# Two layers of cached attention and MLP on one core: most of V's weighting moved from TensorE to VectorE and ScalarE in the first layer

## The chip, the cores and the metric

One core of one Trainium2 chip. The metric is the device time of one execution in microseconds (us). The kernel before takes 677.72 us, the median of three runs (677.35 to 677.88).

## What is computed

One token of width 512 goes through attention, an MLP, the same attention and the same MLP. All weights and caches are float32, and both layers use the same ones.

```
q = (layernorm(x) @ wq) in 32 heads of 128
p = softmax(q . k_cache / sqrt(128)) over 4096 cached positions
o = p . v_cache
x = x + o @ wo
h = gelu(layernorm(x) @ w1 + b1)         # 512 -> 1376
x = x + h @ w2 + b2                      # 1376 -> 512
```

k_cache and v_cache hold 32 heads x 4096 x 128 values, 67 MB each; they don't fit on the core, so each layer reads most of them from HBM.

## The kernel before, in words

**Groups.** The 32 heads go in 8 groups of 4. A group's K and its V are 8.4 MB each (128 partitions x 16,384 values, `BLOCK`), cut into 8 chunks of 2,048 columns (`NC`). Layer 0 takes the groups 0 to 7, layer 1 the groups 7 to 0, so that what lies in SBUF at the end of layer 0 can be used again.

**A group in layer 0** (the loop at L399):
- K is loaded as one transfer, and `scores` (L215) multiplies it with the queries z on TensorE (PE), 8 chunks x 4 heads, all into one PSUM bank, pS.
- `softmax` (L219 to L235) takes maxima and exponentials on VectorE (DVE) and ScalarE (ACT), turns the weights on PE and copies them to `pt` (L229).
- V is loaded as one transfer, and `values` (L243) multiplies it with pt on PE: for each chunk and head the four 128-column blocks of pt against 512 columns of V. Only the diagonal blocks of what comes out in pO are wanted.
- `scaled_out` (L247 to L252) turns pO on DVE, adds up the diagonal blocks and scales.
- `head_out` (L271) multiplies with the group's rows of wo on PE and adds up all groups in one PSUM row, pB.
- `queries` (L205 to L210) makes z of the next group: DVE multiplies the four parts of wq with x and adds them, in place; eight small matmuls sum over the partitions, and a copy puts the result into z.

**Buffers and queues.** All transfers go through SyncE's queue (SP) in program order (`load`, L87); a transfer is issued when its buffer is free, and those behind it wait with it. K and V rotate through three blocks of SBUF: V of a group goes where this group's predecessor had its K, and K of the next group but one goes where this group had its V. wo of a group and wq of the next come as one pair of 2.1 MB into a single place (`PAIR`), behind V; the next pair waits until `queries` and `head_out` have read the old one. Otherwise the framework orders each engine's work by its own estimate of what is ready, except for instructions that `pin` keeps in program order.

**The end of layer 0.** In group 7 V comes in pieces (4, 2, 1 chunks and the last). wo, w1 in two parts and w2 in four follow. `scaled_out_last` treats the last chunk alone. Then comes `mlp`: mean and variance (`mean_of`, `rstd_of`, four small matmuls each), the hidden layer in three thirds (L297; places in PSUM `pH`), a transpose (L309), GELU, and 11 chunks of w2 (L349). The last part of w2 and pieces of layer 1's K and wq are issued behind the chunks of w2 whose places they take (`follow`). `idle` (L374) issues matmuls whose result nobody reads; they keep PE busy where it would wait. `WARM` = 4 of them stand ahead of the hidden layer, and `FILL` = 3 behind the chunks 4 to 7.

Of the kernel before, what the change touches and what calls it, by code (L numbers as in the profile page):

```python
# [17 lines left out]
P = 128  # L18
# [3 lines left out]
G = 8  # L22
# [33 lines left out]
VAR_AT = 1  # L56
WARM = 4


@with_exitstack  # L60
def decode_layers(ctx: ExitStack, tc: tile.TileContext, k, v, w, w1, w2, out):
# [85 lines left out]
    pW = pS[:, 3 * P :], pB[:, :P]  # L147
    pH = (pS, pS[:, P:], pS[:, 2 * P :]), (pS, pB[:, P:], pS[:, P:])
    pM, pN = pO[:, 2 * P : 3 * P], pO[:, 3 * P :]
# [18 lines left out]

    def minus_mean(s, at):
        for j in range(J):  # L170
            nc.tensor.matmul(at[32 * j : 32 * j + 32], negmean.to_broadcast([P, 32]), s, start=True, stop=True)  # L171
        return at

    def mean_of(xs, s, at):
        nm = minus_mean(s, at)
# [5 lines left out]
    def rstd_of(ss, at):  # L181
        nv = minus_mean(ss, at)
# [19 lines left out]

    def queries(n, xc, wt, at, t=None):
        t = wt[:, 0, :] if t is None else t
        pin(nc.vector.tensor_scalar(t, wt[:, 0, :], xc[:, 0:1], None, op0=ALU.mult))  # L205
        for c in range(1, 4):
            nc.vector.scalar_tensor_tensor(t, wt[:, c, :], xc[:, c : c + 1], t, op0=ALU.mult, op1=ALU.add)  # L207
        for j in range(J):
            nc.tensor.matmul(at[:, j : j + 1], t[:, P * j : P * (j + 1)], one, start=True, stop=True)  # L209
        nc.vector.tensor_copy(zq[:, :, C - 1], at[:, :J])  # L210
        return zq
# [29 lines left out]
    def values(i, pt, vt, c, of=C):  # L241
        for j in range(J):
            nc.tensor.matmul(pO[32 * j : 32 * j + 4, :], pt[:, j, c, :], by_head(vt)[:, j],  # L243
                             start=(i == 0), stop=(i == of - 1))

    def scaled_out(rl, ot):
        nc.vector.transpose(ot[:, :512], pO)  # L247
# [3 lines left out]
        nc.vector.tensor_reduce(o, diag, axis=AX.X, op=ALU.add)  # L251
        nc.vector.tensor_scalar(on, o, rl, None, op0=ALU.mult)  # L252
        return on
# [13 lines left out]

    def head_out(on, wt, n):
        for d in range(4):
            if n < G - 1:  # L270
# [12 lines left out]
    def mlp(xs, s, w1_t, w2_t, xb, rows, fill, follow):  # L283
# [7 lines left out]
        def hidden(i):  # L291
            at, first = hs[i], W1_AT[i]
            n = min(32 * HIDDEN[i][1], FJ) - 32 * HIDDEN[i][0]
            for c in range(4):
                for j in range(J):
                    f = first + n * (J * c + j)
                    pin(nc.tensor.matmul(at[32 * j : 32 * j + 2, :n], xs[:, c, :], w1_t[:, f : f + n],  # L297
                                         start=(c == 0), stop=(c == 3)))
                if i == 0 and c == VAR_AT:
                    rstd.append(rstd_of(ss, pN[:, 1:2]))  # L300
                    if fill is None:
                        nc.gpsimd.tensor_tensor(nmr, nm_s, rstd[0], op=ALU.mult)
                        nc.gpsimd.tensor_scalar(cb[:, late:], colsum[:, late:], nmr, None, op0=ALU.mult)
                        nc.gpsimd.tensor_tensor(cb[:, late:], cb[:, late:], b1c[:, late:], op=ALU.add)

# [22 lines left out]
        rstd = []  # L328
        if fill is not None:
            for _ in range(WARM):  # L330
                idle(fill, pO, 2 * P)
# [44 lines left out]
    for layer in range(2):  # L376
        order = list(range(G)) if layer == 0 else list(range(G))[::-1]
        if layer == 0:
            nm, ss, xc = mean_of(xs, s, pN[:, 0:1])
            z = queries(0, xc, wq_first, pO)  # L380
# [12 lines left out]
        xc_l = small("xc_l", 4)  # L393
        r = rstd_of(ss, pN[:, 1:2])
        nc.vector.tensor_copy(xc_l, xc)
# [3 lines left out]
        for n, g in enumerate(order):  # L399
            first, final = n == 0, n == G - 1  # L400

            k_home, v_home = ((2 * n + i) % 3 * BLOCK for i in (1, 2))
# [17 lines left out]
            else:  # L420
                tiles = stream("k", g, HALVES if layer == 1 and final else WHOLE, k_home)
            for c, t in tiles:
# [37 lines left out]
            else:  # L460
                for c, t in stream("v", g, WHOLE, v_home):
                    for i in range(KEPT - 1):
                        if layer == 0 and n == G - 2 and c == (STAY + U * i) // NC:
                            nc.scalar.copy(pK[i], t[:, STAY // U % J + i - J * (c - STAY // NC), :])
                    values(c, pt, t, c)

# [114 lines left out]
```

## Time and profile before

| | us |
|---|---|
| median of three runs | 677.72 |
| the profiled execution | 677.01 |
| its span, first to last instruction | 675.2 |
| busy in it: PE / DVE / ACT | 398.3 / 115.0 / 27.4 |

In the profile PE's weight loads stand apart from its matmuls (PEld), and an f32 matmul shows as two instructions. L215 is line 215 of the kernel. A line of a group tells the engine, what is written and read, the shapes, the count, the busy time, the mean time of one in ns, and the idle time ahead of them with what ended it. The chain of waits follows the work that ended last back to its start. SPq is SyncE's queue: its rows tell when a transfer was issued. The busy time of an engine counts only where others wait for it.

### The profile page before, as it was taken

To read this page: it belongs to the slowest core of one execution; us is meant where nothing else is said; L and a number is where in the kernel's file an instruction comes from. 1 tells how busy PE (TensorE), PEld (TensorE's weight loads), DVE (VectorE), ACT (ScalarE), POOL (GpSimd) and SP (SyncE) were. 2 spreads that over 40 slices of the span, in tenths; PEclk is the share of its full clock that TensorE was granted. 3 is DMA by queue.
4 is the path that set the end of the run, shared out by engine and by line. 5 is a ranking of instruction groups with operands and counts; after the bars stand their busy time and mean duration, and the time that the engine had idled before them with its cause. 6 is when DMAs were issued, how large, how long until landed. Compare 5 with 4: busy or idle time off the path is not lost.

```text
span 675.2 us, 6725 instructions
## 1 busy us (share of the span) xinstructions
PE 398.3 (59%) x3004; PEld 108.3 (16%) x3004; DVE 115.0 (17%) x369; ACT 27.4 (4%) x57; POOL 5.0 (1%) x24
## 2 busy tenths in 40 slices
PE   1544564475545745456498987574355544755697
PEld 1101111111111111111125321111011111111123
DVE  3012110120021201212013322120121011201212
ACT  0010000000000000001011200000000000000010
POOL 1000000000000000000000000000000000000000
PEclk9968876797587856887699998886797678865989
DMA  9999999999999999999999999999999999999996
GB/s 375 435 436 435 436 435 435 413 453 432 427 432 419 447 435 436 431 435 432 417 413 366 393 430 433 432 435 436 431 432 435 433 435 404 451 432 421 432 410 254
DMA packets 10836, 285.34 MB, mean 423 GB/s; under 512 B 1204, under 2 KB 1208, under 8 KB 3384
## 3 DMA queue, kind: packets, MB, share of 16 engines
q1 hardware_dynamic: 10808, 284.92, 98.7%
q8 instruction: 23, 0.38, 0.2%
q14 instruction: 5, 0.04, 0.0%
HBM read 284.92 MB, written 0.00 MB: 422 GB/s over the span
## 4 chain that ended last, share of the span: by engine, by line
PE 41%; DMA 37%; another core or an unknown queue 15%; DVE 4%; ACT 1%; issue 1%; ACTq 0%; SPq 0%; DVEq 0%
DMA arena<-in_v 34%; PE pO L243 19%; PE pS L215 12%; PE pB L271 4%; DMA arena<-in_w 2%; PE pO L209 1%; PE pO L227 1%; PE pS L374 1%; ACT arena L225 1%; DVE smalls L219 1%; DVE arena L247 1%; PE pO L374 1%; PE pO L349 1%; PE pS L297 0%
## 5 line engine op out<-in xcount | busy, mean ns | idle before, releaser
L215 PE MATMUL pS<-arena,smalls 128*8 128x512 f32 x1024 | 141.7, 705 | 121.8 <-DMA arena<-in_k 121.2
L243 PE MATMUL pO<-arena,pt 128*4 128x512 f32 x1008 | 143.3, 710 | 80.7 <-DMA arena<-in_v 80.3
L215 PEld LDWEIGHTS pS<-arena,smalls 128*8 128x8 f32 x1024 | 29.5, 100 | 218.5 <-issue 197.8
L271 PE MATMUL pB<-arena,smalls 128*1 128x512 f32 x112 | 52.0, 608 | 20.1 <-DVE smalls L252 15.9
L243 PEld LDWEIGHTS pO<-arena,pt 128*4 128x4 f32 x1008 | 28.2, 96 | 182.3 <-issue 181.2
L219 DVE TENSOR_REDUCE smalls<-pS 128x1 f32<-128x512 f32 x16 | 11.1, 692 | 255.8 <-PE pS L215 255.8
L247 DVE STREAM_TRANSPOSE arena<-pO 128x512 f32<-128x512 f32 x16 | 11.5, 717 | 220.8 <-PE pO L243 220.8
L227 PE MATMUL pO<-ident,arena 128*128 128x128 f32 x64 | 12.7, 331 | 37.9 <-ACT arena L225 37.6
L225 ACT ACTIVATE arena<-pS,smalls 128x512 f32<-128x512 f32 x16 | 12.4, 778 | 534.8 <-DVE smalls L224 534.8
L207 DVE SCALAR_TENSOR_TENSOR arena<-arena,smalls 128x512 f32<-128x512 f32 x45 | 33.8, 752 | 1.6
L271 PEld LDWEIGHTS pB<-arena,smalls 128*1 128x1 f32 x112 | 8.5, 85 | 63.3 <-issue 35.6
L209 PE MATMUL pO<-smalls,arena 128*128 128x1 f32 x120 | 16.6, 259 | 3.3 <-DVE arena L207 3.3
L209 PEld LDWEIGHTS pO<-smalls,arena 128*128 128x128 f32 x120 | 15.3, 200 | 15.5 <-DVE arena L207 13.8
L227 PEld LDWEIGHTS pO<-ident,arena 128*128 128x128 f32 x64 | 8.2, 163 | 51.8 <-ACT arena L225 46.4
L374 PE MATMUL pS<-arena,ident 128*8 128x512 f32 (+1 forms) x34 | 14.2, 517 | 0.5 <-DVE pt L309 0.5
L374 PE MATMUL pO<-arena,ident 128*8 128x512 f32 (+1 forms) x34 | 12.5, 492 | 0.4 <-DVE smalls L289 0.4
L205 DVE TENSOR_SCALAR arena<-arena,smalls 128x512 f32<-128x512 f32 x15 | 7.2, 480 | 2.8 <-DMA arena<-in_w 2.8
L349 PE MATMUL pO<-arena,smalls 128*1 128x128 f32 x176 | 6.8, 272 | 0.6 <-ACT smalls L323 0.4
L210 DVE COPY smalls<-pO 128x4 f32<-128x4 f32 x15 | 2.5, 165 | 25.7 <-PE pO L209 25.7
L231 DVE STREAM_TRANSPOSE smalls<-smalls 128x32 f32<-128x32 f32 x16 | 3.4, 212 | 17.5 <-ACT arena L225 17.5
L171 PE MATMUL pO<-smalls 128*32 128x1 f32 x64 | 2.2, 184 | 7.0 <-DVE smalls L165 6.5
L297 PE MATMUL pS<-arena,smalls 128*2 128x128 f32 (+1 forms) x160 | 5.2, 259 | 0.5 <-DVE pt L309 0.5
(92 smaller groups left out, 100.9 us busy)
## 6 DMA issues: line engine op xcount, KB each, us to landing
arena<-in_w SPq DMA_DIRECT2D x14, 2048.0 KB, 33.3
arena<-in_k SPq DMA_DIRECT2D x4, 4096.0 KB, 27.8
arena<-in_v SPq DMA_DIRECT2D x2, 4096.0 KB, 38.8
arena<-in_k SPq DMA_DIRECT2D x3, 2048.0 KB, 14.0
arena<-in_v SPq DMA_DIRECT2D x2, 2048.0 KB, 42.0
arena<-in_w SPq DMA_DIRECT2D x4, 1024.0 KB, 15.3
arena<-in_v SPq DMA_DIRECT2D x3, 1024.0 KB, 54.0
arena<-in_w SPq DMA_DIRECT2D x6, 512.0 KB, 10.2
```

The costliest lines, as they stand in the source:

```text
L205: pin(nc.vector.tensor_scalar(t, wt[:, 0, :], xc[:, 0:1], None, op0=ALU.mult))
L207: nc.vector.scalar_tensor_tensor(t, wt[:, c, :], xc[:, c : c + 1], t, op0=ALU.mult, op1=ALU.add)
L209: nc.tensor.matmul(at[:, j : j + 1], t[:, P * j : P * (j + 1)], one, start=True, stop=True)
L215: nc.tensor.matmul(pS[32 * j : 32 * j + C, :], z[:, j, C - 1 - c : 2 * C - 1 - c], kt[:, j, :], start=(c == 0), stop=(c == C - 1))
L219: nc.vector.tensor_reduce(mx[:, 0:1], pS, axis=AX.X, op=ALU.max)
L225: nc.scalar.activation(p, pS, AF.Exp, bias=bias[:, 0:1], scale=sc, accum_out=mx[:, 0:1])
L227: nc.tensor.transpose(pT[:, b].rearrange("p j r -> p (j r)"), p[:, P * b : P * (b + 1)], ident)
L243: nc.tensor.matmul(pO[32 * j : 32 * j + 4, :], pt[:, j, c, :], by_head(vt)[:, j], start=(i == 0), stop=(i == of - 1))
L247: nc.vector.transpose(ot[:, :512], pO)
L271: nc.tensor.matmul(pB[0:1, :], on[:, d : d + 1], wt[:, d, :], start=n == 0 and d == 0, stop=n == G - 2 and d == 3)
L349: pin(nc.tensor.matmul(pM[32 * j : 32 * j + 1, :], g[:, c - b0 : c - b0 + 1], w2_t[c][:, P * j : P * (j + 1)], start=(c == 0), stop=(c == ...
L374: pin(nc.tensor.matmul(at[:C, :n], ident[:, :C], t[:, 0, :n], start=True, stop=True))
```

## The change

- In layer 0, groups 0 to 5, `values` does only the chunks 6 and 7 of V on PE. Chunks 0 to 3 are multiplied by their weights on DVE (one product over 2,048 columns each, in place), chunks 4 and 5 on ACT (32 small products each of 128 columns, 16 a chunk). `add_weighted` sums the six on DVE in one strided reduction, and four matmuls of one row add the result to pO.
- In layer 0, groups 0 to 6, `head_out` sums over wo's four parts on DVE and needs one matmul in place of four.
- In layer 0, from group 0 to 6, `queries` sums over the partitions by one matmul that gives the result on all of them; DVE picks the diagonal by a product with the identity and a reduction. In groups 0 to 5 this comes ahead of the rest of the weighting.
- K of the last group of layer 0 comes in two halves.
- At the start, mean and variance of layer 0 take one matmul each in place of four.
- In the first MLP the variance is computed ahead of the hidden layer, two warming matmuls stand in place of four, and the second third of the hidden layer lies in pO in place of pS.

```
-WARM = 4
+WARM = 2
+VECTOR, SCALAR = 6, 2
...
-    pH = (pS, pS[:, P:], pS[:, 2 * P :]), (pS, pB[:, P:], pS[:, P:])
+    pH = (pS, pO, pS[:, 2 * P :]), (pS, pB[:, P:], pS[:, P:])
...
-    def minus_mean(s, at):
+    def minus_mean(s, at, whole=False):
+        if whole:
+            nc.tensor.matmul(at, negmean.to_broadcast([P, P]), s, start=True, stop=True)
+            return at
...
-    def queries(n, xc, wt, at, t=None):
+    def queries(n, xc, wt, at, t=None, short=False):
...
+        if short:
+            nc.tensor.matmul(at, one.to_broadcast([P, P]), t, start=True, stop=True)
+            own = t.rearrange("p (j d) -> p j d", j=J)
+            nc.vector.tensor_tensor(own, at.rearrange("p (j d) -> p j d", j=J),
+                                    ident[:, None, :].to_broadcast([P, J, P]), op=ALU.mult)
+            nc.vector.tensor_reduce(zq[:, :, C - 1], own, axis=AX.X, op=ALU.add)
+            return zq
...
+    def weighted(pt, at, a, b):
+        own = arena[:, at + NC * a : at + NC * b].rearrange("p (r j d) -> p r j d", j=J, d=DH)
+        for i in range(a, b):
+            t = own[:, 4 * (i - a) : 4 * (i - a + 1)]
+            if i >= vec - SCALAR:
+                for r in range(4):
+                    for j in range(J):
+                        nc.scalar.activation(t[:, r, j], t[:, r, j], AF.Copy, scale=pt[:, j, i, r : r + 1])
+                continue
+            weight = pt[:, :, i, :].rearrange("p j b -> p b j")[:, :, :, None].to_broadcast([P, 4, J, DH])
+            nc.vector.tensor_tensor(t, t, weight, op=ALU.mult)
+
+    def add_weighted(at, n, t):
+        nc.vector.tensor_reduce(t, arena[:, at : at + NC * n].rearrange("p (r m) -> p m r", m=U),
+                                axis=AX.X, op=ALU.add)
+        for j in range(J):
+            nc.tensor.matmul(pO[32 * j : 32 * j + 1, :P], one, t[:, P * j : P * (j + 1)], start=False, stop=True)
...
     def head_out(on, wt, n):
+        if layer == 0 and n < G - 1:
+            t = wt[:, 0, :]
+            nc.vector.tensor_scalar(t, t, on[:, 0:1], None, op0=ALU.mult)
+            for d in range(1, 4):
+                nc.vector.scalar_tensor_tensor(t, wt[:, d, :], on[:, d : d + 1], t, op0=ALU.mult, op1=ALU.add)
+            nc.tensor.matmul(pB[0:1, :], one, t, start=n == 0, stop=n == G - 2)
+            return
...
-                if i == 0 and c == VAR_AT:
+                if i == 0 and c == VAR_AT and fill is None:
                     rstd.append(rstd_of(ss, pN[:, 1:2]))
...
         if fill is not None:
+            rstd.append(rstd_of(ss, pN[:, 1:2]))
             for _ in range(WARM):
                 idle(fill, pO, 2 * P)
...
+            vec = VECTOR if layer == 0 and n < G - 2 else 0
...
-                tiles = stream("k", g, HALVES if layer == 1 and final else WHOLE, k_home)
+                tiles = stream("k", g, HALVES if final else WHOLE, k_home)
...
-                    values(c, pt, t, c)
+                    if c >= vec:
+                        values(c - vec, pt, t, c, C - vec + (vec > 0))
+            if vec:
+                weighted(pt, v_home, vec - SCALAR, vec)
+                weighted(pt, v_home, 0, 2)
...
+            if vec:
+                z = queries(n + 1, xc_l, wq_next, pS, short=True)
+                weighted(pt, v_home, 2, vec - SCALAR)
+                add_weighted(v_home, vec, wq_next[:, 1, :])
             on = scaled_out_last(rl, pt, last_v, others) if final else scaled_out(rl, ot)
...
-            if not final and not (layer == 1 and n == 0):
-                z = queries(n + 1, xc_l, wq_next, pO, ot[:, :U] if layer == 0 and n == G - 2 else None)
+            if not final and not vec and not (layer == 1 and n == 0):
+                z = queries(n + 1, xc_l, wq_next, pO, ot[:, :U] if layer == 0 and n == G - 2 else None, layer == 0)
```

More of the change, by code (lines that the diff above doesn't have):

```diff
@@ L172, in minus_mean, with mean_of @@
         return at
-    def mean_of(xs, s, at):
-        nm = minus_mean(s, at)
+    def mean_of(xs, s, at, whole=False):
+        nm = minus_mean(s, at, whole)
         xc, sq, ss = small("xc", 4), small("sq", 4), small("ss")
@@ L179, in mean_of, with rstd_of @@
         return nm, ss, xc
-    def rstd_of(ss, at):
-        nv = minus_mean(ss, at)
+    def rstd_of(ss, at, whole=False):
+        nv = minus_mean(ss, at, whole)
         ve, r = small("ve"), small("rstd")
@@ L298, in hidden @@
                                          start=(c == 0), stop=(c == 3)))
-                if i == 0 and c == VAR_AT:
+                if i == 0 and c == VAR_AT and fill is None:
                     rstd.append(rstd_of(ss, pN[:, 1:2]))
[L301 to L304, printed above, removed]
+                    nc.gpsimd.tensor_tensor(nmr, nm_s, rstd[0], op=ALU.mult)
+                    nc.gpsimd.tensor_scalar(cb[:, late:], colsum[:, late:], nmr, None, op0=ALU.mult)
+                    nc.gpsimd.tensor_tensor(cb[:, late:], cb[:, late:], b1c[:, late:], op=ALU.add)
         def turned(i):
@@ L378, in decode_layers @@
         if layer == 0:
-            nm, ss, xc = mean_of(xs, s, pN[:, 0:1])
+            nm, ss, xc = mean_of(xs, s, pN[:, 0:1], True)
             z = queries(0, xc, wq_first, pO)
@@ L393, in decode_layers @@
         xc_l = small("xc_l", 4)
-        r = rstd_of(ss, pN[:, 1:2])
+        r = rstd_of(ss, pN[:, 1:2], layer == 0)
         nc.vector.tensor_copy(xc_l, xc)
```

## The prediction

> **What bounds the kernel now.** I read the page's line of DMA first, then the stages by windows, then one group of layer 0 in order of time, then the hand-over from layer 0 to its MLP. The page and the windows (columns: length, busy time of PE, its weight load, DVE, ACT, POOL, then the granted PE clock, the DMA share and GB/s):
>
> ```profile
> span 675.2 us, 6725 instructions
> PE 398.3 (59%) x3004; PEld 108.3 (16%) x3004; DVE 115.0 (17%) x369; ACT 27.4 (4%) x57; POOL 5.0 (1%) x24
> PEclk9968876797587856887699998886797678865989
> DMA  9999999999999999999999999999999999999996
> GB/s 375 435 436 435 436 435 435 413 453 432 427 432 419 447 435 436 431 435 432 417 413 366 393 430 433 432 435 436 431 432 435 433 435 404 451 432 421 432 410 254
> 4.00:340.00 336.00, 176.63 (x1116) 44.26 (x1120) 50.13 (x148) 10.62 (x21) 0.92 (x4) 0.78 1.00 433
> 356.00:384.00 28.00, 25.30 (x396) 12.41 (x396) 10.66 (x47) 3.56 (x8) 1.79 (x6) 1.00 0.97 371
> 660.00:675.20 15.20, 10.62 (x279) 6.11 (x271) 5.03 (x22) 0.62 (x3) 1.50 (x5) 0.96 0.60 238
> ```
>
> From 4 to 340 us, all of layer 0's attention, the 16 DMA engines are full and move 433 GB/s while PE is busy for 177 of 336 us. Bytes are what this kernel pays for. Past the start it gets less than that rate in two places alone: the tail after 660 us, which is layer 1's and stays as it is, and the first MLP with the start of layer 1, where 28 us at 371 in place of 433 GB/s lose 28 x 62/433 = 4.0 us. So a faster layer 0 attention is worth nothing as such, and the most that the edit of the first MLP can bring is 4.0 us.
>
> One group of layer 0 (timeline; start, length):
>
> ```profile
> 44.65 9.36 PE L243 MATMUL pO<-arena,pt 128*4 128x512 f32 x64 [5.85 <-DMA arena<-in_v]
> 55.34 3.59 PE L271 MATMUL pB<-arena,smalls 128*1 128x512 f32 x8 [1.33 <-DVE smalls L252]
> 59.94 0.33 SPq L87 DMA_DIRECT2D arena<-in_w  x1
> 60.32 0.42 SPq L87 DMA_DIRECT2D arena<-in_k  x1
> 69.98 8.65 PE L215 MATMUL pS<-arena,smalls 128*8 128x512 f32 x64 [10.06 <-DMA arena<-in_k]
> 78.70 0.69 DVE L219 TENSOR_REDUCE smalls<-pS 128x1 f32<-128x512 f32 x1 [18.59 <-PE pS L215]
> 82.16 0.25 DVE L229 COPY pt<-pO 128x128 f32<-128x128 f32 x1
> 89.34 3.60 PE L243 MATMUL pO<-arena,pt 128*4 128x512 f32 x16 [7.30 <-DMA arena<-in_v]
> ```
>
> V of group 0 is there at 44.65, V of group 1 at 89.34: a period of 44.7 us here, about 43.6 in the mean (18.9 MB at 433 GB/s). At 59.94 SP issues the next pair of wo and wq, once the queries have released the old pair; behind it in the same queue stands the next K but one, which overwrites this group's V. Both then wait their turn behind V of group 1, which lands 29 us later. That lead is the cover under which the first half of the change moves.
>
> **The change, part by part.** The prices (columns: busy us, mean ns of one, idle before):
>
> ```profile
> L207 DVE SCALAR_TENSOR_TENSOR arena<-arena,smalls 128x512 f32<-128x512 f32 x45 | 33.8, 752 | 1.6
> L205 DVE TENSOR_SCALAR arena<-arena,smalls 128x512 f32<-128x512 f32 x15 | 7.2, 480 | 2.8 <-DMA arena<-in_w 2.8
> L219 DVE TENSOR_REDUCE smalls<-pS 128x1 f32<-128x512 f32 x16 | 11.1, 692 | 255.8 <-PE pS L215 255.8
> L222 DVE TENSOR_REDUCE smalls<-smalls 128x1 f32<-128x8 f32 x16 | 2.6, 161 | 0.6
> L251 DVE TENSOR_REDUCE smalls<-arena 128x4 f32<-128x16 f32 x16 | 2.9, 179 | 0.5
> L247 DVE STREAM_TRANSPOSE arena<-pO 128x512 f32<-128x512 f32 x16 | 11.5, 717 | 220.8 <-PE pO L243 220.8
> L252 DVE TENSOR_SCALAR smalls<-smalls 128x4 f32<-128x4 f32 x16 | 3.7, 230 | 0.6
> L165 DVE SCALAR_TENSOR_TENSOR smalls<-pt,smalls 128x4 f32<-128x4 f32 x3 | 0.5, 163 | 0.1
> L165 DVE SCALAR_TENSOR_TENSOR smalls<-arena 128x4 f32<-128x4 f32 x1 | 0.2, 164 | 3.1 <-DMA arena<-in_w 3.1
> L464 ACT COPY pK<-arena 128x512 f32<-128x512 f32 x5 | 2.7, 582 | 7.9 <-DMA arena<-in_v 7.9
> L323 ACT ACTIVATE smalls<-smalls 128x4 f32<-128x4 f32 (+1 forms) x6 | 1.2, 207 | 37.6 <-DVE smalls L322 36.6 <-DVE smalls L317 1.0
> ```
>
> *Groups 0 to 5, counted from the landing of V.* L219 against L222: 504 more elements for 531 ns, so 1.05 ns an element over a fixed 0.15 us. No row shows a product of two SBUF tensors of 2,048 elements. By that slope a weighted chunk is 0.15 + 2,048 x 1.05 ns = 2.3 us; the upper bound is four of L207, 3.0 us. I take 2.3, since a slope drops the fixed part that L207 carries each time.
> - Chunks 0 and 1 on DVE: 4.6 us. By then wo and wq have come (2.1 MB, 4.8 us after V); wait 0.3.
> - Queries: 0.48 + 3 x 0.752 = 2.74, as before. The one product over all 512 columns is two of L271's eight instructions, 3.59/4 = 0.9, and takes the place of the eight small ones; then a product with the identity and a reduction over 512 elements, 2 x 0.7 = 1.4, in place of a small copy. z comes 1.2 us later than it could, but K of the next group lands only at +25 (69.98 less 44.65): no cost. Were K early, it would cost those 1.2 us.
> - Chunks 2 and 3: 4.6.
> - Chunks 4 and 5 on ACT beside that: 32 instructions of 128 elements. Between 207 ns (4 elements) and 582 ns (512) that is about 0.30 each, 9.6 us; at 582 each, 18.6. DVE asks for them at +14.6, so nothing, or 4 us at the bound.
> - The sum over six chunks, 12,288 elements whose neighbours lie 2,048 bytes apart. This is the disputed cost, R. At 1.05 ns it is 12.9 us. The nearest strided row is L251, which reads 16 elements 516 bytes apart in 179 ns where eight adjacent ones take 161: if the whole excess over a fixed 153 ns lies in the elements, 1.6 ns each and R = 20; if the eight further ones carry it, 18/8 = 2.25 ns and R = 27.6. Against that, L165 takes 163 ns with a strided first input (x3) and 164 with an adjacent one. And L251 writes four results where L222 writes one, which may be its excess. I take 12.9, by L165.
> - Four small matmuls 0.4, then L247, L251 and L252, 1.1; wo as a chain on DVE 2.74 and one product 0.9, against 3.59 on PE before.
>
> Sum: 4.6 + 0.3 + 2.7 + 0.9 + 1.4 + 4.6 + R + 0.4 + 1.1 + 2.7 + 0.9 = 19.6 + R = 32.5 us. So SP issues the next pair at 44.65 + 32.5 = 77.2 in place of 59.94, with K but one behind it. Who waits? Nobody, while V of group 1 is still coming, until 89.3. The deadline: a piece of w2 below, issued into a nearly empty queue, takes 4.8 us for 0.79 MB, that is 1.8 us of bytes and 3.0 of way. So the pair must be issued by 89.3 - 3.0 = 86.3, which is 41.6 after V: R may be 22.0 us. DVE itself: its part ends at +31.6, the next softmax (78.70 to 82.41, 3.7 us) begins at +34 and ends at +38, the next V comes at +44.7. Both fit, with 9 and 6 us to spare. PE, relieved of 48 of 64 value matmuls, gains nothing, because it waits for DMA on both sides.
>
> [...]
>
> *Group 6* keeps its values on PE. Its wo chain comes ahead of the queries on DVE, so z(7) is ready at about 326 instead of 323; K of group 7, now in two halves, has its first at 332.08 - 9.7 = 322.3.
>
> *The end of layer 0* (chain of waits; then two loads by issue and landing):
>
> ```profile
> 332.08 9.06 PE pS L215 x64
> 341.17 0.70 DVE smalls L219
> 358.01 0.33 DVE pt L504
> 359.24 1.49 PE pO L374 x7
> 361.14 0.99 PE pS L297 x29
> 363.58 0.87 PE pO L349 x32
> 367.87 1.30 PE pS L374 x6
> 369.19 0.84 PE pO L349 x24
> ```
>
> ```profile
> L87 SPq DMA_DIRECT2D arena<-in_w x1: 431/431/431, 322.3 to 322.3; - x1
> DMA to landing us min/median/max: 37.9/37.9/37.9
> L87 SPq DMA_DIRECT2D arena<-in_w x1: 328/328/328, 364.3 to 364.3; - x1
> DMA to landing us min/median/max: 4.8/4.8/4.8
> ```
>
> With the halves, 32 scores are done before K's end and only half remains: 4.5 us of the 9.06 go. But V's pieces and wo come when they come. wo comes 2.1 MB, 4.8 us, ahead of w1's first part, which lands at 322.3 + 37.9 = 360.2; wo is there at 355.4, and 32 small matmuls like those of L297 (0.99) follow, so L504 can't start before about 356.4, against 358.01: 1.6 us gained. The hidden layer's first third needs w1: 360.3 instead of 361.14, 0.8 us. Two warming matmuls fewer and the variance ahead of them cost nothing, since PE waits for w1 there. The second third, now in another PSUM bank, doesn't wait for the transpose; but w2's first megabyte lands 2.4 us behind w1, at 362.6, so L349 starts 0.8 us earlier. Its end releases the last part of w2 (issued 364.3, landed 369.1), also 0.8 earlier. Now the rest of w1 (0.7 MB, at 364.3) and w2's next two pieces (0.5 MB each, to 366.7) are late in its place. These were issued in time before and are bound by bytes; PE used them as they came. So the next chunks end at 367.8, and the six filling matmuls hold PE till 367.8 + 1.3 = 369.1, against 369.19. **0.1 us is left of 0.8.**
>
> *The start* loses six tiny matmuls while K's 8.4 MB are coming: nothing.
>
> Sum against the profiled run, 677.01 us (span 675.2, 1.8 around it): 677.01 - 0.1 = 676.9. The median of the three runs, 677.72, lies 0.7 above the profiled one, so the forecast is **677.6**. Some 0.2%, 1.35 us, is what can be told from no change.
>
> **The rivals.**
> *DVE overruns (slower, 0.20).* If the strided sum takes over 22 us, 1.8 ns an element, the pair of weights is issued into an empty queue, and from then DVE sets the period. For: L251's 2.25. Against: L165's 163. At R = 27.6 the chain is 47.2 us; the first gap is 47.2 - 41.6 = 5.6. Then DVE goes from its end (0.9 us before the issue) through the softmax into the next V: a period of 47.2 - 0.9 + 3.7 = 50.0 against 43.6, five times 6.4. Together 38 us: 715. At R = 24: 2.0 + 5 x 2.8 = 16: 694.
> *The clock drops in the MLP (0.10).* Fewer warming matmuls leave PE nearly idle from 358 to 360. The page's PEclk falls to 5 to 8 in slices where PE waits for DMA. At half clock the matmuls from L297 to L349 (0.99, as much again and 0.87) cost 2.9 us more, less the 0.8 gained: up to +2.1, 678.6 to 679.8. Decides if the clock falls between 357 and 361.
> *The MLP's gain holds (faster, 0.10).* If DMA uses the earlier issues to refill a third to all of the 4.0 us: 676.3 down to 673.7. Against: the chain above, bound by landings and fillers.
>
> **How the numbers follow.** Forecast 0.60, at 677.6 give or take 0.5. Faster by over 0.2%: the third rival, 0.10. Slower: the first, 0.20, and 0.04 of the second above 679.1. Within: 0.60 and 0.06. The range starts at 675.7, half of the 4.0 us won back, and goes to 682.0, over the second rival's end and an overrun of 0.7 us in each of six groups (R = 22.7). Outside stay 0.03 below and 0.17 of the overrun above.
>
> **What would show it.** The strided reduction: 12.9 us for one (about 20 would still pass, 27 not). DVE some 275 us busy in place of 115 (26 us in each of six groups), PE about 340 (398, less 48 x 0.146 = 7.0 in each of six groups and 2.7 in each of seven heads). SP issues of the pair near 77, then every 43.6 us; V of the groups landing as before; 433 GB/s from 4 to 340. Scores of group 7 end near 336; L504 near 356.4; L297 at 360.3; the last L349 still near 369.1. A gap in GB/s inside layer 0 would make me wrong on DVE, an L349 ending before 368.5 on the MLP.

## The result and the profile after

| | before | after |
|---|---|---|
| median | 677.5 (676.94 to 677.88, 6 runs) | 725.65 (724.41 to 728.35, 6 runs) |
| ratio, 95% interval | | 1.0715 [1.0703, 1.0727] |
| profiled execution, its span | 677.01, 675.2 | 728.35, 725.9 |

The change costs 48 us. The forecast was no change, 677.6 us in a range of 675.7 to 682.0; the measured time lies 44 us above that range.

The page of after: its span, busy times, GB/s by slice, the share of each engine in the chain of waits, the two groups that carry the loss, and the products on ACT (line numbers from here on are those of the kernel that the rows belong to; scores are now L226, values on PE L254, softmax starts at L230):

```profile
span 725.9 us, 6315 instructions
PE 353.3 (49%) x2664; PEld 93.2 (13%) x2664; DVE 316.1 (44%) x434; ACT 84.0 (12%) x249; POOL 5.0 (1%) x24
GB/s 406 404 460 408 415 438 451 185 473 408 232 415 448 177 460 408 231 456 354 255 433 409 315 391 430 436 420 444 441 423 441 407 457 420 444 423 423 431 413 235
DVE 35%; DMA 34%; PE 28%; issue 2%; ACT 1%; ACTq 0%; DVEq 0%; SPq 0%
L272 DVE TENSOR_REDUCE arena<-arena 128x512 f32<-128x12288 f32 x6 | 124.1, 20678 | 0.0
L275 PE MATMUL pO<-arena,smalls 128*1 128x128 f32 x48 | 7.1, 395 | 171.8 <-DVE arena L272 171.8
L265 ACT ACTIVATE arena<-arena,pt 128x128 f32<-128x128 f32 x192 | 56.7, 387 | 12.6 <-DMA arena<-in_v 7.0 <-DVE pt L240 5.5
```

The row of GB/s was level in layer 0 and now has five holes, of 177 to 255. One strided sum takes 20.7 us, and over the six groups PE stands 172 us ahead of the four small products of each group that add its result to pO. From here on "the sum" is `add_weighted`'s on DVE, "the sum's products" are these four matmuls, and "the head's product" is the one matmul of `head_out`.

One group of after in order of time, from V of group 0 to V of group 1 (start, length, ..., the idle time ahead):

```profile
44.51 6.70 DVE L268 TENSOR_TENSOR arena<-arena,pt 128x2048 f32<-128x2048 f32 x3 [5.75 <-DMA arena<-in_v]
53.72 1.53 DVE L211 SCALAR_TENSOR_TENSOR arena<-arena,smalls 128x512 f32<-128x512 f32 x2
55.17 20.68 DVE L272 TENSOR_REDUCE arena<-arena 128x512 f32<-128x12288 f32 x1
75.77 0.74 DVE L211 SCALAR_TENSOR_TENSOR arena<-arena,smalls 128x512 f32<-128x512 f32 x1
76.56 2.07 PE L213 MATMUL pS<-arena,smalls 128*128 128x512 f32 x2
79.91 0.65 DVE L217 TENSOR_REDUCE smalls<-arena 128x4 f32<-128x512 f32 x1
83.84 1.01 PE L305 MATMUL pB<-arena,smalls 128*1 128x512 f32 x1 [4.69 <-DVE arena L304]
84.67 9.76 PE L226 MATMUL pS<-arena,smalls 128*8 128x512 f32 x61
85.74 0.33 SPq L88 DMA_DIRECT2D arena<-in_w  x1
94.52 0.69 DVE L230 TENSOR_REDUCE smalls<-pS 128x1 f32<-128x512 f32 x1 [10.73 <-PE pS L226]
98.26 2.29 DVE L268 TENSOR_TENSOR arena<-arena,pt 128x2048 f32<-128x2048 f32 x1
...
139.49 0.33 SPq L88 DMA_DIRECT2D arena<-in_w  x1
351.37 0.33 SPq L88 DMA_DIRECT2D arena<-in_w  x1
```

Two things are not where the prediction had them. The last step of the queries (L211 at 75.77) stands behind the sum, so z is ready at 80.6 (end of L217). And the next group's scores begin at 83.9, with the head's product (L305), although their K, behind the same bytes, had come by 69.98 in before. They end at 94.4, the softmax follows, and the weighting of V, which landed at 89.3, starts at 98.26. Weighting, sum, head, scores and softmax are one row, that is, each waits for the one ahead of it: 53.75 us from 44.51 to 98.26. SP issues the pair at 85.74 and, five groups later, at 351.37: (351.37 - 85.74)/5 = 53.1 us a group in place of 43.6. Five times 9.5 us are 47.5, of a loss of 48.

### The profile page after: what moved, and what is told of

Same layout as the page of the kernel before. It is cut to its first block, busy times and chain, and to the rows that moved or that the text cites. A ratio compares the mean times of both kernels' runs of the same rounds, so it can differ in the third digit from the quotient of the medians.

```text
span 725.9 us, 6315 instructions
## 1 busy us (share of the span) xinstructions
PE 353.3 (49%) x2664; PEld 93.2 (13%) x2664; DVE 316.1 (44%) x434; ACT 84.0 (12%) x249; POOL 5.0 (1%) x24
## 4 chain that ended last, share of the span: by engine, by line
DVE 35%; DMA 34%; PE 28%; issue 2%; ACT 1%; ACTq 0%; DVEq 0%; SPq 0%
DMA arena<-in_v 32%; DVE arena L272 17%; PE pO L254 10%; PE pS L226 10%; DVE arena L268 7%; DMA arena<-in_w 2%; DVE arena L211 2%; DVE arena L304 2%; PE pS L213 2%; PE pB L305 2%; PE pS L412 1%; DVE smalls L230 1%; PE pO L387 1%; DVE arena L215 1%; DVE arena L278 1%
## 5 line engine op out<-in xcount | busy, mean ns | idle before, releaser
L226 PE MATMUL pS<-arena,smalls 128*8 128x512 f32 x1024 | 146.4, 699 | 55.6 <-DMA arena<-in_k 53.5
L254 PE MATMUL pO<-arena,pt 128*4 128x512 f32 x720 | 105.4, 711 | 44.0 <-DMA arena<-in_v 41.1
L272 DVE TENSOR_REDUCE arena<-arena 128x512 f32<-128x12288 f32 x6 | 124.1, 20678 | 0.0
L230 DVE TENSOR_REDUCE smalls<-pS 128x1 f32<-128x512 f32 x16 | 11.1, 692 | 194.9 <-PE pS L226 194.9
L236 ACT ACTIVATE arena<-pS,smalls 128x512 f32<-128x512 f32 x16 | 12.4, 777 | 521.7 <-DVE smalls L235 521.7
L278 DVE STREAM_TRANSPOSE arena<-pO 128x512 f32<-128x512 f32 x16 | 11.4, 713 | 123.2 <-PE pO L254 123.2
L265 ACT ACTIVATE arena<-arena,pt 128x128 f32<-128x128 f32 x192 | 56.7, 387 | 12.6 <-DMA arena<-in_v 7.0
L268 DVE TENSOR_TENSOR arena<-arena,pt 128x2048 f32<-128x2048 f32 x24 | 53.9, 2285 | 5.8 <-DMA arena<-in_v 5.8
L226 PEld LDWEIGHTS pS<-arena,smalls 128*8 128x8 f32 x1024 | 29.7, 97 | 157.7 <-issue 135.5
L211 DVE SCALAR_TENSOR_TENSOR arena<-arena,smalls 128x512 f32<-128x512 f32 x45 | 33.7, 749 | 1.1
L254 PEld LDWEIGHTS pO<-arena,pt 128*4 128x4 f32 x720 | 19.6, 95 | 113.1 <-issue 108.2
L309 PE MATMUL pB<-arena,smalls 128*1 128x512 f32 x56 | 26.9, 625 | 10.8 <-DVE smalls L283 6.6
L305 PE MATMUL pB<-arena,smalls 128*1 128x512 f32 x14 | 12.4, 988 | 32.4 <-DVE arena L304 32.4
L304 DVE SCALAR_TENSOR_TENSOR arena<-arena,smalls 128x512 f32<-128x512 f32 x21 | 15.8, 751 | 0.7
L238 PEld LDWEIGHTS pO<-ident,arena 128*128 128x128 f32 x64 | 7.3, 150 | 51.9 <-ACT arena L236 46.5
L213 PE MATMUL pS<-arena,smalls 128*128 128x512 f32 x12 | 12.5, 1141 | 0.4
```

The costliest lines, as they stand in the source:

```text
L213: nc.tensor.matmul(at, one.to_broadcast([P, P]), t, start=True, stop=True)
L226: nc.tensor.matmul(pS[32 * j : 32 * j + C, :], z[:, j, C - 1 - c : 2 * C - 1 - c], kt[:, j, :], start=(c == 0), stop=(c == C - 1))
L238: nc.tensor.transpose(pT[:, b].rearrange("p j r -> p (j r)"), p[:, P * b : P * (b + 1)], ident)
L265: nc.scalar.activation(t[:, r, j], t[:, r, j], AF.Copy, scale=pt[:, j, i, r : r + 1])
L268: nc.vector.tensor_tensor(t, t, weight, op=ALU.mult)
L272: nc.vector.tensor_reduce(t, arena[:, at : at + NC * n].rearrange("p (r m) -> p m r", m=U), axis=AX.X, op=ALU.add)
```

## The experiments

Three theories stand in the first expectations. The first, the row (A): the next group's scores stand on PE behind the weighted sum and the head, so that the steps of a group can't overlap. The second, the queries (B): only the late z costs. The third, VectorE's work (C): the added work is too much in any order. The deadline in what follows is the prediction's estimate: the pair of the first group has to be issued by 86.3 us, or DMA runs dry; how far ahead of it the pair comes is the lead. Unless something else is said, a kernel computes the whole reference.

**The price of the strided sum.** The kernel before, with one more reduction over the 12,288 values of V in each of the groups 0 to 5; its result is not used.

```
+            if layer == 0 and n < 6:
+                src = arena[:, v_home : v_home + 6 * NC]
+                view = (src.rearrange("p (m r) -> p m r", m=1), src.rearrange("p (r m) -> p m r", m=U),
...
+                pin(nc.vector.tensor_reduce(made, view, axis=AX.X, op=ALU.add))
```

> The kernel before, with one more reduction on DVE in each of the groups 0 to 5, in the time in which DVE is idle behind the queries; it reads 12,288 values of V and its result is not used. Group 0: all adjacent, one result. Group 1: 512 results of 24 adjacent values. Group 2: 512 results of 24 values 2,048 bytes apart, as in the change. Groups 3, 4, 5: 512 results of 24 values 8, 16 and 32 bytes apart. The prediction's price (1.05 ns an element) gives 12.9 us for all six. If distance costs, as the shape of the four diagonal blocks suggested (1.6 ns an element), groups 0 and 1 take 12.9 and group 2 takes 20.7, and the other three tell from which distance on. If the number of results costs, groups 1 to 5 all take about 20.7 and group 0 takes 12.9. The time of the kernel should stay within 1 us of before, since DMA is ahead by 29 us.

In the kernel the groups 1 and 2 are the other way round than the expectation says. By group: all adjacent with one result; 24 values 2,048 bytes apart for each of 512 results; 24 adjacent; 8 bytes apart; 16; 32. The timeline of this kernel, start and length:

```profile
59.05 12.94 DVE L511 TENSOR_REDUCE arena<-arena 128x1 f32<-128x12288 f32 x1
105.45 21.17 DVE L511 TENSOR_REDUCE arena<-arena 128x512 f32<-128x12288 f32 x1
147.76 12.94 DVE L511 TENSOR_REDUCE arena<-arena 128x512 f32<-128x12288 f32 x1
191.78 12.94 DVE L511 TENSOR_REDUCE arena<-arena 128x512 f32<-128x12288 f32 x1
235.78 22.17 DVE L511 TENSOR_REDUCE arena<-arena 128x512 f32<-128x12288 f32 x1
279.78 22.31 DVE L511 TENSOR_REDUCE arena<-arena 128x512 f32<-128x12288 f32 x1
```

Distance is the price: 12.94 us, 1.05 ns an element, at 4 and 8 bytes; 22.17 and 22.31 us, 1.8 ns, at 16 and 32; 21.17 us, 1.7 ns, at 2,048. The number of results cost nothing: 12.94 us for one as for 512. The step lies between 8 and 16 bytes; what makes it, the rows don't show. The time was 677.41 us (one run): 13 to 22 us more of DVE in each group, with nobody waiting, cost nothing. That speaks against the third theory.

**z early.** After, with the query steps, the weighting of the chunks 2 and 3 (`between`), the two last steps of the queries and the strided sum pinned on DVE in this order.

```
-            nc.vector.scalar_tensor_tensor(t, wt[:, c, :], xc[:, c : c + 1], t, op0=ALU.mult, op1=ALU.add)
+            pin(nc.vector.scalar_tensor_tensor(t, wt[:, c, :], xc[:, c : c + 1], t, op0=ALU.mult, op1=ALU.add))
...
+            if between is not None:
+                between()
```

> The changed kernel with one edit: on DVE the queries of the next group, with their product and the diagonal, are put ahead of the strided sum, which stays as it is (20.7 us in the changed kernel's trace); the order on PE is left to the framework, and there the four matmuls that add the weighted sum, and the head's, still stand ahead of most of the next group's scores. Theory of the row (A): the period of a group in layer 0, 53.1 us between two issues of the weight pair, is one chain in which the next scores on PE stand behind the sum and the head; an early z alone doesn't break it. It expects the last scores of a group to end where they did, about 50 us after the landing of V, and 715 to 726 us. Theory of the queries (B): the scores start late only because z is late (80.5 us in the first group, behind the sum). It expects scores at the landing of K, a period near 43.6 and 677 to 682 us. Theory of DVE's work (C): the sum costs too much in any order, over 700 us here and in every kernel with this sum.

717.09 us (one run), 8.6 less than the median of after. z is ready some 20 us ahead of the sum's end, and the scores still wait, as the timeline of PE shows (L277 adds the sum, L307 is the head's product):

```profile
131.76 0.61 PE L277 MATMUL pO<-arena,smalls 128*1 128x128 f32 x8 [24.24 <-DVE arena L274]
132.14 1.91 PE L228 MATMUL pS<-arena,smalls 128*8 128x512 f32 x2
136.57 1.01 PE L307 MATMUL pB<-arena,smalls 128*1 128x512 f32 x1 [2.52 <-DVE arena L306]
137.39 8.12 PE L228 MATMUL pS<-arena,smalls 128*8 128x512 f32 x59
```

The second theory (677 to 682) falls; the first (715 to 726) holds.

**PE's order alone.** After, with the next group's scores put ahead of the sum's four products on PE, z as late as in after.

```
+                for c, t in stream("k", order[n + 1], WHOLE, (2 * n + 3) % 3 * BLOCK):
+                    scores(z, c, t)
+                done = True
                 add_weighted(v_home, vec, wq_next[:, 1, :])
```

> The changed kernel with PE's order mended alone: the next group's scores ahead of the four matmuls that add the weighted sum; on DVE the last step of the queries stays behind the strided sum. Theory of the row (A): z comes 36 us after V as before, so the scores end about 10 us later, the softmax follows, and the period is about 50 us in place of 53.1: 715 to 721 us. So neither order alone gives the 40 us that both give together. If PE's order alone were the cause: 677 to 685.

729.09 us (one run): both expectations missed. The row is only turned round: scores at 132.65, then the sum's products at 141.38, then the next softmax's transposes, and the head's product behind them at 146.36. So the pair is issued for the first time at 96.38, past the deadline of 86.3, and then every 51.9 us.

**Both orders.** The two edits together (query steps early on DVE, scores ahead of the sum's products on PE), the strided sum unchanged.

> The changed kernel with its strided sum, and both orders mended: on DVE the queries ahead of the sum, and on PE the next group's scores ahead of the four matmuls that add the weighted sum. Theory of the row (A): scores run beside the sum from the landing of K, DVE's own work is about 4.6 + 2.7 + 4.6 + 1.4 + 20.7 + 1.1 + 2.7 + 3.7 = 41.5 us a group, under 43.6; the weight pair is issued about 40.5 us after V, just inside the 41.6 of the prediction: 677 to 681 us. Theory of the queries (B): the same as its first run, no further gain from PE's order. Theory of DVE's work (C): over 700 us.

682.88 us (681.99 to 684.85), ratio 1.0076 [1.0058, 1.0094]: 43 of the 48 us are back, with the same instructions. The third theory (over 700) falls; the first asked for 677 to 681 and missed by 2. The timeline of PE:

```profile
98.76 2.08 PE L213 MATMUL pS<-arena,smalls 128*128 128x512 f32 x2 [5.65 <-DVE arena L211]
115.34 9.43 PE L228 MATMUL pS<-arena,smalls 128*8 128x512 f32 x64 [14.50 <-DMA arena<-in_k]
125.56 0.40 PE L277 MATMUL pO<-arena,smalls 128*1 128x128 f32 x8 [0.80 <-DVE arena L274]
128.90 0.66 PE L240 MATMUL pO<-ident,arena 128*128 128x128 f32 x4 [2.94 <-ACT arena L238]
130.16 1.65 PE L307 MATMUL pB<-arena,smalls 128*1 128x512 f32 x2 [0.60 <-DVE arena L306]
```

The scores now start with K and run beside the sum, which took 21.16 us from 104.35. The pair is issued 42 us after V landed, at the end of the lead. The head's product now stands behind the next softmax's transposes (L240), but that isn't what holds it: it and the sum's products wait last for DVE (0.60 and 0.80 us). What is left is DVE's own chain with its sum of 21 us.

**A short sum.** After, with the strided sum written as additions of neighbours (five of 2,048 at 2.28 us, one of 1,024, one of 512: 13.3 us).

```
-        nc.vector.tensor_reduce(t, arena[:, at : at + NC * n].rearrange("p (r m) -> p m r", m=U), axis=AX.X, op=ALU.add)
+        v0 = arena[:, at : at + NC]
+        for c in range(1, n):
+            nc.vector.tensor_tensor(v0, v0, arena[:, at + NC * c : at + NC * (c + 1)], op=ALU.add)
+        nc.vector.tensor_tensor(v0[:, : 2 * U], v0[:, : 2 * U], v0[:, 2 * U :], op=ALU.add)
+        nc.vector.tensor_tensor(t, v0[:, :U], v0[:, U : 2 * U], op=ALU.add)
```

> The changed kernel with the strided sum replaced by seven additions of adjacent columns: five of 2,048, one of 1,024, one of 512, by 2.29 us for 2,048 (the weighting's row in the changed kernel) 11.4 + 1.2 + 0.7 = 13.3 us in place of 20.7. Orders are left to the framework. Theory of the row (A): the chain of 53.1 us gets 7.4 shorter, 45.7, still over 43.6; five periods give 5 x 7.4 and the first group some more: 683 to 690 us. Theory of the queries (B): z still waits behind the additions in part, some us gained, over 690. Theory of DVE's work (C): DVE is relieved of 7.4 us a group and fits: 677 to 680.

677.75 us (one run): the first theory missed. It left out the lead: the pair is issued at 76.8 for the first time, 9.5 us ahead of its deadline, and a period 1.1 us too long takes up only 5.5 of it in five groups. The same kernel, timed:

> The changed kernel with its one strided sum (20.7 us) written as five additions of 2,048 neighbouring values, one of 1,024 and one of 512 (13.3 us), nothing else; the full result. One run of it gave 677.75, beside 677.5 before the change. Theory "serial chain" (sum, head, next scores and softmax follow one another in each group, so that the period is 31 us and the sum's duration): the period is 44.5 us instead of 43.6 while the transfers wait, the pair's lead of 9.5 us takes that up over five groups, and the time is that of before: 676.8 to 678.2. Theory "the work on VectorE costs something in any order": 678.5 to 680.

677.15 us (676.73 to 678.06), ratio 1.0004 [0.9995, 1.0013]: one instruction of the change, written in another way, gives the whole 48 us back, in the framework's own order. The row is still there, as the timeline of PE says (L278 adds the sum, L308 is the head):

```profile
114.84 0.60 PE L278 MATMUL pO<-arena,smalls 128*1 128x128 f32 x8 [7.78 <-DVE arena L276]
119.64 1.01 PE L308 MATMUL pB<-arena,smalls 128*1 128x512 f32 x1 [4.20 <-DVE arena L307]
120.47 9.98 PE L226 MATMUL pS<-arena,smalls 128*8 128x512 f32 x61
133.22 0.66 PE L238 MATMUL pO<-ident,arena 128*128 128x128 f32 x4 [2.77 <-ACT arena L236]
```

It fits, since the sum is 7.4 us shorter and, being seven instructions, lets the query steps in between: z is ready at 112.9, 23.7 us after V, where it was at 36.

**Both orders and the short sum.**

> The changed kernel with both orders mended and the seven additions of adjacent columns in place of the strided sum. Theory of the row (A): DVE's own work is 34 us a group, the weight pair is issued about 33 us after V with 8 us to spare in every group, so DMA never runs dry: the time of the run with V's weighting on PE, 677.0 to 677.8. If the work on DVE and ACT costs something by itself (slower transfers, a lower rate in layer 0): over 679.

681.57 us (680.34 to 682.28), ratio 1.0055 [1.0043, 1.0068], against an expected 677.0 to 677.8. It lies where the expectation's other theory has it (over 679, the work on DVE and ACT costs something by itself), but the same work in the framework's order took 677.15, so that isn't the reason. The mended order is worse than the framework's once the sum is short, and moves the pair's first issue from 76.8 to 84.1. The timeline of one group shows where: the last addition (L278) ends at 116.4, but the sum's products (L280) stand behind the scores and start at 122.38, 5.9 us later; the head's product (L310) follows and waits last for DVE.

```profile
115.75 0.69 DVE L278 TENSOR_TENSOR arena<-arena 128x512 f32<-128x512 f32 x1
122.38 0.40 PE L280 MATMUL pO<-arena,smalls 128*1 128x128 f32 x8
127.36 1.64 PE L310 MATMUL pB<-arena,smalls 128*1 128x512 f32 x2 [0.60 <-DVE arena L309]
```

In this profile the granted clock also fell in the MLP, as two windows show (after the busy times: clock, DMA share, GB/s); it was 1.00 there in before and in the run of both orders:

```profile
360.00:364.00 4.00, 2.24 (x36) 1.13 (x40) 0.69 (x7) 0.00 (x0) 0.76 (x2) 0.89 0.96 399
364.00:368.00 4.00, 3.50 (x84) 2.36 (x78) 1.54 (x6) 0.41 (x2) 0.19 (x1) 0.68 0.99 398
```

**A longer sum.** The short sum with one or two (`range(2)`) more instructions of 2.28 us in its chain (15.6 and 17.9 us).

```
+        for _ in range(1):
+            nc.vector.tensor_tensor(v0, v0, v0, op=ALU.max)
```

> As the additions, with one more instruction of 2.28 us in the chain of each of the six sums (the greater of a value and itself over 2,048 values, which changes nothing in the result), so that the sum takes 15.6 us. Theory "serial chain": the period is 46.8 us, 3.2 above the transfers' 43.6; the pair is issued at 79.05 for the first time, with 7.2 us of lead to its deadline at 86.3; five periods lose 16 us, so 8.8 are left over: 684 to 689. Theory "the pair's deadline alone" (the prediction's: a sum of up to 22 us passes): 677 to 678.5. Theory "a straight line" from 677.75 at 13.3 us to 725.65 at 20.7 us, with no lead to use up: 691 to 694.

> As the run before it, with two such instructions, so that the sum takes 17.9 us. Theory "serial chain": period 49.1 us, 5.5 above 43.6; lead 4.9 us; five periods lose 27.4, so 22.5 are left over: 697 to 703. Theory "the pair's deadline alone": 677 to 678.5. Theory "a straight line": 706 to 709.

One more: 682.52 us (682.41 to 685.24), ratio 1.0096 [1.0079, 1.0113], 1.5 below the row's range, with a period of 46.0 us. Two more: 678.06 (677.25 to 679.12), ratio 1.0018 [1.0008, 1.0027], where the row asked for 697 to 703. More work made it faster, so the row as stated there failed. The trace shows why: the framework had given PE another order. In after and in all runs up to here with the scores behind the sum, the head's product (here L310) comes ahead of nearly all scores; in this one it comes behind 21 of the 64 instructions of the scores:

```profile
119.90 0.61 PE L280 MATMUL pO<-arena,smalls 128*1 128x128 f32 x8 [12.43 <-DVE arena L278]
120.28 5.16 PE L226 MATMUL pS<-arena,smalls 128*8 128x512 f32 x21
125.21 0.59 PE L310 MATMUL pB<-arena,smalls 128*1 128x512 f32 x1
125.70 4.82 PE L226 MATMUL pS<-arena,smalls 128*8 128x512 f32 x40
133.29 0.66 PE L238 MATMUL pO<-ident,arena 128*128 128x128 f32 x4 [2.77 <-ACT arena L236]
```

**The head's place alone.** The same kernel with two more instructions, the head's product pinned ahead of the first score product of a group:

```
-            nc.tensor.matmul(pB[0:1, :], one, t, start=n == 0, stop=n == G - 2)
+            pin(nc.tensor.matmul(pB[0:1, :], one, t, start=n == 0, stop=n == G - 2))
...
+            if layer == 0 and j + c == 0:
+                pin(ins)
```

> The run with two more instructions in the sum (17.9 us) kept 678.06 against "serial chain", which gave 697 to 703; its trace has PE begin 21 of the next group's scores before the head's product, where the run with one more had 2. Here the head's product is pinned ahead of all of those scores on PE; the work, its sizes and VectorE's order stay, and the result is the full one. Theory "the head's place on PE": every group waits some 4 us for the head before its scores, so that the period is the 46.8 us of the run with one more and 2.3 for the longer sum, 49.1 us; lead 4.9 us, five periods lose 27.4: 697 to 703. Theory "the order on PE costs nothing, a sum of 17.9 us passes the pair's deadline": 677 to 679.

701.71 us (701.26 to 703.41), ratio 1.0367 [1.035, 1.0384]: 23.7 us for the place of one product.

```profile
123.27 0.60 PE L282 MATMUL pO<-arena,smalls 128*1 128x128 f32 x8 [12.43 <-DVE arena L280]
128.07 1.01 PE L312 MATMUL pB<-arena,smalls 128*1 128x512 f32 x1 [4.20 <-DVE arena L311]
128.90 8.46 PE L226 MATMUL pS<-arena,smalls 128*8 128x512 f32 x61
140.13 0.66 PE L240 MATMUL pO<-ident,arena 128*128 128x128 f32 x4 [2.77 <-ACT arena L238]
```

From the sum's products to the next transposes it is 16.9 us here (123.27 to 140.13) and 13.4 there (119.90 to 133.29): PE waits 4.20 us for the head's factor while K (landed at 113.4) and z (116.7) lie ready. And the other way, the kernel with z early (717.09) and the head behind 12 of 32 scores:

> The changed kernel with its strided sum (20.7 us) and the queries pinned early, as in the run that gave 717.09, and on PE the head's product now behind 12 of the next group's 32 score products instead of 1; nothing else, and the full result. Theory "the head's place on PE": the wait of about 4 us between sum and scores goes, the period falls from 51.4 to 47.5 us, five periods give back 19.5: 695 to 701; what stays above before is that the scores still stand behind the sum's own products. Theory "it is the sum, wherever the head stands": 715 to 718. Theory "PE's order was all of it": 677 to 680.

697.47 us (696.13 to 698.3), ratio 1.0295 [1.028, 1.031], 19.6 less than with the head in front. Both as the head's place asked. In the run with the head first, with K and z there, none of the scores began ahead of the waiting product: it started at 128.07, the first score at 128.09.

**All of them by one sum.** What five periods have above 43.6 us, less the lead to 86.3 at the pair's first issue, on top of 677.5 where that is positive (us). First issue and period are read from each run's trace, so the table accounts for the times; it doesn't say what makes a period long.

| kernel | first issue | period | sum gives | measured |
|---|---|---|---|---|
| after | 85.7 | 53.1 | 724.6 | 725.65 |
| z early | 86.4 | 51.4 | 716.4 | 717.09 |
| PE's order alone | 96.4 | 51.9 | 729.0 | 729.09 |
| z early, head later | 84.3 | 47.6 | 695.7 | 697.47 |
| both orders | 85.5 | 44.9 | 683.2 | 682.88 |
| short sum | 76.8 | 44.7 | 677.5 | 677.15 |
| short sum, both orders | 84.1 | 44.6 | 680.1 | 681.57 |
| one more | 79.2 | 46.0 | 682.6 | 682.52 |
| two more | 81.5 | 44.5 | 677.5 | 678.06 |
| two more, head first | 81.4 | 48.7 | 698.0 | 701.71 |

Some 2 of the last line's 3.7 us lie around the first MLP: from 369.81 to 399.81 its DMA moved 341 GB/s, and 371 in the same stretch of "z early, head later" (367.47 to 397.47), which over 30 us is 2.1 us of 433 GB/s. Why, and what the rest is, stays open.

**The rest of the change.** After, with the weighting taken out (values all on PE again); wo's sum, the short queries, the halves and the edits of the first MLP stay.

```
-VECTOR, SCALAR = 6, 2
+VECTOR, SCALAR = 0, 0
```

> The changed kernel with V's weighting given back to PE (all eight chunks in the value matmuls, nothing on DVE or ACT); everything else of the change stays: the head on DVE, the queries by one product, the last K in halves, the first MLP. Theory of the row (A): none of the 48 us lies in these parts, 677.0 to 677.6; the first MLP gives 0.1 to 0.4 us, since the hidden layer starts earlier but the filling matmuls behind the seventh chunk hold PE. If the other parts had a share in the loss: over 679.

678.44 us (677.32 to 679.4), ratio 1.0009 [1.0000, 1.0018]: no gain, 0.8 above the upper end of what was expected, and below the 679 from which the other parts would have had a share in the loss. The timeline of PE, the hidden layer (L335) and the last chunks of w2 (L387):

```profile
327.38 9.54 PE L226 MATMUL pS<-arena,smalls 128*8 128x512 f32 x64 [1.50 <-DVE smalls L217]
360.43 1.05 PE L335 MATMUL pS<-arena,smalls 128*2 128x128 f32 x32 [0.78 <-DMA arena<-in_w]
369.18 0.84 PE L387 MATMUL pO<-arena,smalls 128*1 128x128 f32 x24
```

The same with one filling matmul in place of three behind the chunks 4 to 7:

> The kernel of the run above (V's weighting on PE), with one filling matmul in place of three behind the chunks 4 to 7 of the first MLP's second product. If the prediction's account of the MLP is right, these fillers hold the last three chunks until about 369.1 us, while their weights could be there at 368.4: 0.5 to 0.8 us less than the run above, 676.4 to 676.9. If the landing of the weights holds them, no difference within 0.2 us.

677.56 us (676.71 to 678.92), ratio 1.0002 [0.9992, 1.0011], 0.9 below the one before it and level with before, where the expectation's two theories asked for 0.5 to 0.8 less or for no difference within 0.2.

```profile
369.09 0.84 PE L387 MATMUL pO<-arena,smalls 128*1 128x128 f32 x24 [0.96 <-DMA arena<-in_w]
```

With fewer fillers PE waits for the last part of w2 instead, and starts 0.09 us earlier: the landing of these bytes bounds this stage, whoever fills the wait, as the second theory has it. So of the 0.9 us between the two medians this stage has 0.09; the rest is not accounted for.

## Why the prediction was wrong

- **The step that failed** is "DVE itself: its part ends at +31.6, the next softmax (...) begins at +34 and ends at +38, the next V comes at +44.7. Both fit". The softmax's start at +34 was read from before, where PE was free when K came. With the change PE holds, in its order, the sum's products and the head's ahead of the scores, and the softmax began at +50.0 (94.52 less 44.51), and the next weighting, behind it, at +53.75, 9 us after V had landed. "PE (...) gains nothing, because it waits for DMA on both sides" took PE for idle where it had become the place at which all must pass. The short sum (13.3 us, near the 12.9 taken) shows that even at the forecast price the row is as long as the period (44.7 against 43.6); only the lead hid it. The runs that moved nothing but the order show that the order makes the row: with the strided sum kept, both orders give back 43 of the 48 us, and with a sum of 17.9 us the place of the head's product alone is worth 23.7.
- **"z comes 1.2 us later than it could (...): no cost"** counted DVE's steps in the order of the text, z at about +10. The framework put one query step behind the sum, and z came at +36. Pinning it gave back 8.6 us alone, and PE's order alone gave nothing (729.09); together they gave 43.
- **The price R**, 12.9 by L165, was 20.7. The price went with the distance: 12.94 us for adjacent values, 21.17 for values 2,048 bytes apart. L165 was too short to show it: by an estimate from these two rows, 0.7 ns more an element, its four elements would show some 3 ns. L251's lower reading, 1.6 ns an element, gave 20. The right price alone would not have mended the forecast: "about 20 would still pass" was the wrong bound, as it looked at the pair's issue only.
- **What held.** The chain: 19.6 + 20.7 = 40.3 us from V to the pair's issue by the prediction's sum, 41.2 measured (the same steps in another order). The deadline 86.3: the pair came at 85.74. A weighted chunk: 2.3 us against 2.285. ACT: 9.6 us taken for a group's 32 instructions, 9.45 measured (56.7 for six groups; the mean of one, 387 ns, is longer because they overlap: 32 of them end to end would be 12.4 us), hidden. One product for the queries took 2.07 us instead of 0.9, at a granted clock of 0.50 from 76 to 79 us.
- **The rivals.** "DVE overruns" came nearest, with 694 to 715 us, but its condition was not met (R below 22, the pair in time), and its period left out the scores: with R = 20.7 its sum, 40.3 - 0.9 + 3.7, gives 43.1 us, below the 43.6 of the transfers, where 53.1 were measured; the scores take 9.8 of the difference. That its time came nearest is luck. The granted clock did fall in the MLP in one profile (0.68 in both orders with the short sum), and was 1.00 in that of the rest of the change. "The MLP's gain holds" is refuted by the last two runs.
- **The MLP** came out at the times worked out, in the run of the rest alone: scores of group 7 end at 336.9 (forecast 336), the hidden layer starts at 360.43 (360.3), the last chunks at 369.18 (before: 369.19). The reason given was only in part right: w2's last part was to land 0.8 us earlier and the fillers to hold PE. It was issued 0.4 to 0.5 us earlier (363.92 and 363.79 against 364.29), but with fewer fillers PE still waited for its landing until 369.09.

What stays open: why the two orders together still lose 5.4 us (4.4 with the short sum, against the short sum alone). The traces point to the late pair. With the strided sum DVE's own chain brings it to the deadline; with the short sum its products wait 5.9 us behind the scores. A pair that is issued late also lands late, and then the queries wait for it: DVE waits for wo and wq at the queries seven times, for 8.6 us (7.6 with the short sum), where after and the short sum alone have one such wait, of 2.8 and 2.1 us. No run moved any of this alone. That the order costs the time is shown by the runs; that the framework's own estimate of the sum's time chose that order was only argued, and not tried.

## What to carry to other kernels

When work moves from one engine to another, list what stands behind its result in the queue of the engine that uses it. PE, busy for 49% of the span of after, was a serial gate here: with a sum of 17.9 us it waited 4.20 us at the head's product while the scores behind it had K and z, and that order took 701.71 us in place of 678.06. Ask of each stage not only whether the next transfer is issued in time, but whether the whole row (result, next scores, next softmax) fits into the period (in after 53.1 us against 43.6), and count how many periods a lead can pay for (with the short sum 9.5 us of lead paid for five periods, each 1.1 us too long). Where a framework orders the queues, read the order that it made before trusting a sum of durations.

## What the hardware showed

A reduction on DVE over 12,288 f32 values took 12.94 us, 1.05 ns an element, with neighbours 4 and 8 bytes apart, and 21.17 to 22.31 us, 1.7 to 1.8 ns, at 16, 32 and 2,048 bytes. Seven adjacent additions that write 11,776 elements in all took 13.3 us, less than the one strided instruction's 20.7 us over 12,288.
